# Third-term slices on GpSimd, two more dummy matmuls, folds in sequence and a new order in a two-branch attention kernel

## The chip, the core and the metric

The kernel runs on one core of a Trainium2 chip. The core has five engines with a queue each: TensorE (PE in the profile, its weight loads PEld), VectorE (DVE), ScalarE (ACT), GpSimd (POOL) and SyncE (SP, which here issues nearly all DMAs). They share no order but the semaphores that the program sets. The metric is the device time of one execution in microseconds. Three runs of the kernel before took 785.99, 787.32 and 787.73 us; their median is 787.32.

## What is computed

Two attention layers read the same input x (2048 tokens, 640 features, 32 heads of 20) and are mixed by a gate for each token. Branch A is full softmax attention. In branch B a token sees only the 8 tokens at distances 0, 2, ..., 14 behind it.

```python
g = sigmoid((x * gate_w).sum(-1, keepdims=True))
# A, for each of 32 heads:
p = softmax(q @ k.T * 20**-0.5);  a = (p @ v) joined over the heads @ A_wo
# B, for each head: 8 keys per token, at pos - 0, 2, ..., 14
attn = softmax(q . k[pos - off] * 20**-0.5);  b = (attn . v[pos - off]) joined @ B_wo
out = g * a + (1 - g) * b
```

## The kernel before, in words

**Tiling.** Branch A is cut into 32 groups: 4 chunks of 512 queries (`qc`) by 8 sets of 4 heads (`q`). A group has 16 blocks of 128 keys for each of its 4 heads, so 64 units, each a score block of 128 keys by 512 queries; there are 2048 units in all. `qk` (L1933) lets PE compute the scores of two or three units into PSUM, and `exp` (L1951) lets ScalarE turn these into exponentials in `ebuf` in one instruction; that is a tile, and a step `s` of the main loop. `pv` (L1996) multiplies exponentials by the values (with a column of ones, for the softmax's sum) and accumulates a whole group in the PSUM bank `obank`; four units, one of each head, run side by side in PE.

**Rides: exponentials on VectorE.** Some units do not go to ScalarE. They are taken in quads of up to four (one block of keys, 4 heads). `wanted` decides whether a tile takes such a ride along, or `lone` sends one alone. VectorE then makes a first integer from the score (`clamp`, L1910, result `uD`), whose bits read as bfloat16 are an approximate exponential. To sharpen it, it is summed from K = 4 terms: the term `k` is `uD` plus the constant `SHIFTS[k]` = 0, 32, 64, 96, multiplied by values that are scaled with `WEIGHTS[k]`. The first term is `uD` itself. The other three, k = 1, 2, 3 (second, third and fourth term), are written into slots of `eD`, a ring of `NS` = 3 slots: `gen_d` (L1018, its instruction is L1036) adds the constant on VectorE for all units of a quad at once, one instruction a term. The scaled values `vS` are made on GpSimd (L1082). So a ride costs PE four products in `pv` in place of one. A slot is free again once `pv` has read it.

**Slices on GpSimd.** `piece` (L1050, its instruction is L1065) may take one unit's slice of the second term (k = 1) off VectorE: GpSimd adds the constant as a 32-bit integer addition of `two`, a tile whose one constant, `SHIFTS[1] * 65537`, adds 32 to both 16-bit halves. `pdone` lists which units of a quad are done so, `pshut` remembers that `gen_d` has begun the second term of a quad, so that it is too late for more. `piece` is called by `slot`, after an instruction of VectorE of at least 0.59 us (in the planner's numbers) that reads PSUM or otherwise leaves alone the SBUF port that VectorE shares with GpSimd. If some other work of GpSimd waits for such a slot (`gen_vs`, the norm of a finished group, taps of branch B when `PTAPS` asks for them), that goes first. `last_port` orders the GpSimd instruction behind VectorE's last one that needs the port.

**Side work.** Projections, branch B (`gen_bproj`, `gen_b`), the gate, the norms and the output products are generators. `spend` runs them in the time that PE has left between tiles, through three PSUM banks (`side`), and `filler` (L2017) puts dummy products where PE would be idle. `gen_fold` (L1470) multiplies both branches' results of half a query chunk by the output weights, copies them from PSUM to `outsb` (L1483, L1491) and issues the DMA to the output (L1496). It starts when branch B's half, the output weights and all 8 norms of the chunk are done. There are six; the last chunk goes another way. `close` forces the two folds of the chunk two before to be done.

**What sets the order.** While the program is built, a planner (`_Sched` and the loop at the end of `_build`) keeps an estimated clock for each engine and writes each engine's queue; the waits follow from what is read and written. It decides by 21 settings, which `PLAN` replaces at given steps: slack and tolerances, priorities of the side work, how far VectorE may run ahead, when a ride is taken, and `PTAPS`.

**The head.** `HEAD` is a string that lists the first operations: `t` transposes two blocks of x on PE (L1626), `x` and `y` copy these to SBUF on ScalarE and VectorE (L1636, L1640), `a`, `b`, `k` project the first keys (L1646), and so on up to the first scores. Ahead of it seven dummy matmuls into `obank` (L581) run on zeros.

Of the kernel before, what the change touches and what calls it, by code (L numbers as in the profile page):

```python
# [52 lines left out]
    0: ((0.326, 0.478), 0.16, 1, 1.79, 0.79, -1.26, -0.25, 11.51, 2.0, 9.43, 0.45, 0.67, 3.16, 3.61, -0.03, 0.59, 1, -5.33, 0.3, -1.0, (0, 2)),  # L53
    5: ((0.326, 0.478), 0.16, 1, 1.79, 0.79, -1.26, -0.25, 11.51, 2.0, 9.43, 0.4, 0.67, 3.16, 3.61, -0.03, 0.59, 1, -5.33, 0.3, -1.0, (0, 2)),
    10: ((0.326, 0.478), 0.16, 1, 1.79, 0.79, -1.26, -0.25, 11.51, 3.71, 8.58, 0.4, 0.67, 3.16, 3.61, -0.03, 0.59, 1, -5.33, 0.3, -1.0, (0, 2)),
    15: ((0.381, 0.757), 0.16, 1, 6.06, 0.79, -1.26, -0.25, 11.51, 3.71, 8.58, 0.91, 0.67, 5.31, 4.07, -0.03, 0.59, 2, -5.33, 0.3, -1.0, (0, 2)),
    20: ((0.381, 0.757), 0.16, 2.46, 6.06, 0.79, -1.26, -0.25, 11.51, 3.71, 7.95, 0.91, 0.67, 5.31, 4.07, -0.03, 0.59, 2, -5.33, 0.3, -1.0, (0, 2)),
    25: ((0.381, 0.757), 0.16, 2.46, 6.06, 0.79, -1.26, -0.25, 11.51, 3.71, 6.0, 0.91, 0.67, 5.31, 2.7, -0.03, 0.59, 1, -5.33, 0.3, -1.0, (0, 2)),
    35: ((0.34, 0.55), 0.16, 1.0, 1, 0.69, -1.26, -0.43, 7.8, 4.71, 6.0, 0.91, 0.49, 5.31, 4.29, -0.03, 0.59, 1, -5.33, 0.3, -1.0, (2, 0)),
    40: ((0.34, 0.55), 0.16, 1.0, 1, 0.64, -1.26, -0.43, 7.8, 4.71, 6.0, 0.91, 0.2, 6.33, 4.29, 0.03, 0.59, 1, -5.33, 0.3, -1.0, (2, 2)),  # L60
    45: ((0.34, 0.55), 0.16, 1.0, 1, 0.64, -1.26, -0.13, 7.8, 4.71, 6.0, 0.91, 0.2, 6.33, 4.29, 0.03, 0.59, 1, -5.33, 0.3, -1.0, (2, 2)),
    50: ((0.34, 0.55), 0.16, 1.0, 1, 0.75, -1.26, -0.13, 7.8, 4.71, 6.0, 0.91, 0.2, 6.33, 4.29, 0.03, 0.59, 1, -5.33, 0.3, -1.0, (2, 2)),
    55: ((0.34, 0.55), 0.16, 1.0, 1, 0.75, -1.27, -0.34, 7.8, 4.71, 6.0, 0.91, 0.2, 6.33, 4.29, 0.03, 0.59, 1, -5.33, 0.3, -1.0, (2, 2)),
    60: ((0.421, 0.553), 0.16, 1.0, 1, 0.76, -1.27, -0.34, 7.8, 4.71, 6.0, 0.91, 0.2, 6.33, 4.29, 0.03, 0.59, 1, -5.33, 0.3, -1.0, (2, 2)),
    65: ((0.421, 0.553), 0.16, 1.0, 1, 0.76, -1.27, -0.34, 7.8, 4.71, 6.0, 0.91, 0.2, 6.33, 4.29, 0.1, 0.59, 1, -5.33, 0.3, -1.0, (2, 2)),
    75: ((0.421, 0.553), 0.16, 1.0, 1, 0.76, -1.27, -0.34, 7.8, 1, 6.0, 0.91, 0.2, 6.33, 4.29, 0.1, 0.59, 1, -5.33, 0.3, -1.0, (2, 2)),
    85: ((0.421, 0.553), 0.16, 1.0, 1, 1.14, -1.27, -0.34, 7.8, 7.0, 6.0, 0.91, 0.2, 7.07, 4.29, 0.1, 0.59, 1, -5.33, 0.3, -1.0, (2, 2)),
    95: ((0.421, 0.553), 0.16, 1.0, 1, 1.14, -1.27, -0.34, 7.8, 7.0, 6.0, 0.91, 0.2, 7.07, 4.29, 0.0, 0.59, 1, -5.33, 0.3, -1.0, (2, 2)),
    100: ((0.34, 0.51), 0.39, 1, 1.0, 0.89, -1.26, -0.43, 7.8, 7.0, 9.43, 0.91, 0.32, 5.31, 4.07, 0.08, 0.59, 2, -6, 0.3, -1.0, (2, 2)),
    105: ((0.34, 0.51), 0.25, 1, 1.0, 0.89, -1.26, -0.43, 7.8, 8, 5.03, 0.91, 0.32, 5.31, 3.77, 0.08, 0.59, 2, -6, 0.3, -1.0, (2, 2)),  # L70
    110: ((0.34, 0.51), 0.25, 1, 1.0, 0.89, -1.26, -0.43, 6.8, 8, 5.03, 0.91, 0.32, 5.31, 3.77, 0.08, 0.59, 2, -6, 0.3, -1.0, (2, 2)),
    115: ((0.29, 0.69), 0.25, 1, 1.0, 1.21, -1.26, -0.43, 6.8, 8, 8.57, 0.56, 0.59, 4.37, 3.61, 0.08, 0.73, 2, -3.49, 0.3, -1.0, (2, 2)),
    120: ((0.291, 0.715), 0.39, 1.0, 1.0, 0.94, -1.6, -0.92, 5.92, 2.0, 4.68, 0.64, 0.65, 4.56, 4.29, 0.0, 0.65, 2, -3, 0.3, -1.0, (2, 2)),
    125: ((0.291, 0.715), 0.39, 1.0, 1.0, 0.94, -1.6, -0.92, 5.92, 2.0, 4.68, 0.64, 0.57, 4.56, 4.29, 0.0, 0.65, 2, -3, 0.3, -1.0, (2, 2)),
    130: ((0.291, 0.715), 0.39, 1.0, 1.0, 0.94, -1.6, -0.92, 2, 2.0, 4.68, 0.64, 0.57, 4.56, 4.29, 0.0, 0.65, 2, -3, 0.3, -1.0, (2, 2)),
    140: ((0.291, 0.715), 0.39, 1.0, 1.0, 0.94, -1.6, -0.92, 2, 1, 4.68, 0.53, 0.57, 4.56, 4.29, -0.03, 0.65, 2, -3, 0.3, -1.0, (2, 2)),
    145: ((0.291, 0.715), 0.39, 1.0, 1.0, 1.17, -1.6, -0.92, 2, 1, 4.68, 0.53, 0.57, 4.56, 4.29, -0.03, 0.65, 2, -5.3, 0.3, -1.0, (2, 2)),
    150: ((0.291, 0.715), 0.39, 1.0, 1.0, 1.17, -1.6, -0.92, 2, 1, 4.68, 0.56, 0.57, 4.56, 4.29, -0.03, 0.65, 2, -5.3, 0.3, -1.0, (2, 2)),
# [339 lines left out]
def _build(ctx, nc, A_x, A_wqkv, A_wo, B_wqkv, B_wo, gate_w, out):  # L418
# [66 lines left out]
    kmd4 = small[:, 6:10]  # L485
    KMd = sb([P, CN, 32], BF16, "KMd")
    zero = sb([P, 32], BF16, "zero")
    two = sb([P, 1], I32, "two")
    vw = sb([P, 4], BF16, "vw")
    onesrow = sb([P, 1], FP32, "onesrow")  # L490
    ones2 = sb([P, 2], BF16, "ones2")
# [526 lines left out]
    def gen_d(d):  # L1018
# [6 lines left out]
        for k in range(1, K):  # L1025
# [7 lines left out]
            if k == 1:  # L1033
                pshut[0] = d
# [10 lines left out]
    last_port = lambda: [sch.last_port] if sch.last_port else []  # L1045

    pdone = []
    pshut = [-1]

    def piece(t0):  # L1050

        for d in range(max(0, len(dquads) - 2), len(dquads)):
            if d <= pshut[0] or (closed[d] and not ridden[d]):
                continue
# [1175 lines left out]
```

## Time and profile before

| what | value |
|---|---|
| median of three runs | 787.32 us |
| the profiled execution | 787.67 us |
| its span, first to last instruction | 785.8 us |
| granted clock of PE, mean | 0.999 |
| first exponential starts | 19.74 us |
| tiles (exponential instructions of ScalarE) | 707 |
| rides (clamps of VectorE) | 419 |
| slices of the second term on GpSimd | 182 |

A row of the groups reads: line, engine, operation, what is written from what, shape, number of instructions; after the first bar the busy time in us (overlaps counted once) and the mean duration in ns; after the second the idle time of that engine just before these instructions and what ended it. A row of the timeline reads: start, length in us, then the same. A mean in ns can be longer than an instruction's share of a full engine, since consecutive instructions overlap by about 0.1 us.

### The profile page before, as it was taken

How to read it: one execution, taken by the hardware profiler on the slowest of the kernel's cores; microseconds unless marked ns; L12 is line 12 of the kernel's file. 1: busy time of each engine (PE TensorE's matmuls, PEld its weight loads, DVE VectorE, ACT ScalarE, POOL GpSimd, SP SyncE). 2: the span in 40 equal slices, each digit the busy share in tenths (PEclk: the TensorE clock that was granted, in tenths of full speed). 3: DMA queues.
4: the chain of work that ended last, by engine and by line, in shares of the span. 5: the costliest groups of instructions: out<-in, count | busy, mean ns of one | idle time of the engine just before them, and what ended most of it. 6: DMA issues, size and time to landing. Idle time of an engine off the chain costs nothing.

```text
span 785.8 us, 30107 instructions
## 1 busy us (share of the span) xinstructions
PE 751.9 (96%) x12482; PEld 293.4 (37%) x12483; DVE 699.5 (89%) x1245; ACT 762.3 (97%) x746; POOL 270.4 (34%) x465
## 2 busy tenths in 40 slices
PE   8999999999999999999999999999999999999997
PEld 5432333322233343233334433433343334335333
DVE  5689888999999989997889999999899899996993
ACT  4999999999999999999999999999999999999995
POOL 4124323333543334223334332423234343442220
PEclk9999999999999999999999999999999999999999
DMA  7321221011121142431112401431421241141421
GB/s 228 111 63 39 61 56 37 20 40 28 33 71 35 36 118 54 96 88 29 49 49 66 90 26 54 87 78 33 109 59 28 52 109 43 36 110 41 89 50 35
DMA packets 71454, 49.88 MB, mean 63 GB/s; under 512 B 43096, under 2 KB 64872, under 8 KB 71320
## 3 DMA queue, kind: packets, MB, share of 16 engines
q1 hardware_dynamic: 71032, 47.64, 24.1%
q8 instruction: 99, 1.62, 0.9%
q14 instruction: 35, 0.29, 0.1%
q10 hardware_dynamic: 288, 0.33, 0.1%
HBM read 32.79 MB, written 7.62 MB: 51 GB/s over the span
## 4 chain that ended last, share of the span: by engine, by line
PE 48%; ACT 25%; DVE 14%; issue 12%; DMA 1%; POOL 1%; SPq 0%; DVEq 0%; ACTq 0%; POOLq 0%
ACT ebuf L1951 25%; PE score L1933 14%; PE obank L1996 13%; PE side L685 13%; DVE uD L1910 5%; PE score L685 4%; DVE eD L1036 2%; DVE kvw L1309 1%; DVE qkvB L1138 1%; DMA oTd<-in_A_x_dram 1%; DVE kvw L1200 1%; PE score L1626 1%; PE side L1321 1%; PE score L2017 1%; DVE qkvB L732 0%
## 5 line engine op out<-in xcount | busy, mean ns | idle before, releaser
L1951 ACT ACTIVATE ebuf<-score 128x1024 bf16<-128x1024 f32 (+1 forms) x707 | 749.5, 1207 | 5.2 <-PE score L1933 4.0
L1910 DVE TENSOR_SCALAR uD<-score 128x512 int16<-128x512 f32 x419 | 279.2, 682 | 27.8 <-PE score L1933 26.7
L1933 PE MATMUL score<-qT,kT 32*128 32x512 bf16 x1856 | 257.8, 384 | 17.9 <-ACT ebuf L1951 12.4
L1036 DVE TENSOR_SCALAR eD<-uD 128x2048 int16<-128x2048 int16 (+3 forms) x298 | 185.2, 644 | 4.4 <-PE obank L1996 4.0
L1065 POOL TENSOR_TENSOR eD<-uD,two 128x256 int32<-128x256 int32 x182 | 110.2, 615 | 131.9 <-DVE eD L1036 56.0
L1996 PE MATMUL obank<-ebuf,vA 128*21 128x512 bf16 x1629 | 153.6, 385 | 1.1 <-ACT ebuf L1951 0.7
L1933 PEld LDWEIGHTS score<-qT,kT 32*128 32x128 bf16 x1856 | 63.7, 91 | 210.5 <-ACT ebuf L1951 141.6
L1996 PE MATMUL obank<-eD,vS 128*21 128x512 bf16 x1257 | 109.6, 379 | 0.0
L1082 POOL TENSOR_TENSOR vS<-vA,vw 128x252 bf16<-128x252 bf16 x105 | 65.5, 624 | 124.5 <-DVE eD L1036 54.7
L685 PE MATMUL side<-xT,wBs 128*32 128x256 bf16 x2220 | 89.6, 281 | 1.5 <-DVE rQ L1275 0.7
L685 PEld LDWEIGHTS side<-xT,wBs 128*32 128x32 bf16 x2220 | 63.2, 142 | 28.4 <-issue 15.0
L1008 POOL TENSOR_TENSOR oN<-oTt,oN 128x256 bf16<-128x256 f32 x60 | 44.2, 737 | 74.2 <-DVE eD L1036 49.5
L1996 PEld LDWEIGHTS obank<-ebuf,vA 128*21 128x21 bf16 x1629 | 36.7, 89 | 85.0 <-issue 61.3
L993 POOL TENSOR_TENSOR rcp<-rcp,gA 128x16 f32<-128x16 f32 x30 | 6.7, 223 | 125.7 <-DVE eD L1036 89.6
L1200 DVE TENSOR_TENSOR kvw<-qkvB 128x2048 bf16<-128x2048 bf16 (+2 forms) x40 | 45.2, 1164 | 0.1
L1138 DVE CAST qkvB<-side 128x512 bf16<-128x512 f32 (+1 forms) x67 | 39.1, 593 | 6.3 <-PE side L685 5.9
L1309 DVE TENSOR_TENSOR kvw<-kvw,eB 128x2048 bf16<-128x2048 bf16 (+1 forms) x40 | 44.1, 1118 | 0.6 <-DMA eB<-scr_e 0.6
L1996 PE MATMUL obank<-uD,vA 128*21 128x512 bf16 x419 | 40.8, 379 | 0.0
L1996 PEld LDWEIGHTS obank<-eD,vS 128*21 128x21 bf16 x1257 | 30.8, 91 | 17.6 <-issue 1.6
L685 PE MATMUL side<-xT,WqP 128*32 128x512 bf16 x380 | 29.5, 383 | 0.7 <-DVE xT L1346 0.5
L685 PE MATMUL side<-xT,kvw 128*32 128x512 bf16 (+1 forms) x360 | 29.1, 383 | 0.6 <-DVE oB L732 0.3
L685 PE MATMUL side<-kvw,xT 128*32 128x160 bf16 (+1 forms) x760 | 28.3, 262 | 1.1 <-DVE vA L911 0.4
(207 smaller groups left out, 592.0 us busy)
## 6 DMA issues: line engine op xcount, KB each, us to landing
kvw<-scr_v SPq DMA_DIRECT2D x32, 336.5 KB
oN<-scr_n SPq DMA_DIRECT2D x60, 128.0 KB
scr_v<-qkvB SPq DMA_DIRECT2D x32, 85.0 KB
wBs<-in_B_wqkv_dram SPq DMA_DIRECT2D x5, 480.0 KB
WqP<-in_A_wqkv_dram SPq DMA_DIRECT2D x14, 160.0 KB
oTd<-oN SPq DMA_DIRECT2D x108, 20.0 KB
out_dram<-outsb SPq DMA_DIRECT2D x12, 160.0 KB
qT<-dst SPq DMA_DIRECT2D x93, 20.0 KB
```

The costliest lines, as they stand in the source:

```text
L685: ins = e.matmul(o[j:k, :], l(j) if callable(l) else l[:, j:k], r, start=(first and i == 0), stop=(last and i == n - 1), skip_group_check= ...
L1008: T("pool", 0.73, lambda e, cols=cols: e.tensor_tensor(oN[0][:, cols], oTt[:, cols], rcpR[:, cols], ALU.mult), reads=["oTt", "oN%d" % i], ...
L1036: T("dve", 0.065 + 0.1334 * (n - m), lambda e, k=k, sl=sl, m=m: e.tensor_scalar(eD[:, sl % NS, 512 * m:512 * n].bitcast(I16), uD[d % 2][:, ...
L1065: T("pool", PDUR, lambda e: e.tensor_tensor(eD[:, sl % NS, 512 * i:512 * (i + 1)].bitcast(I32), uD[d % 2][:, 512 * i:512 * (i + 1)].bitcas ...
L1082: T("pool", 0.607, lambda e: e.tensor_tensor(vS[:, d % 2, :, :], _ap(vA, (kb * NQ + q) * 4 * DV, [[0, K - 1], [1, 4 * DV]]), _ap(vw, 0, [[ ...
L1138: t = TB(dvc(n * TOK), lambda e, o=o, i=i: e.tensor_copy(o, i), reads=[("side", b)], writes=[key])
L1200: TB(dvc(n_ * TOK, 2), lambda e: e.tensor_tensor(o, i0, i1, ALU.mult), reads=["qB", "kB"], writes=prods(i, range(n_)) + olds(), port=True)
L1309: TB(dvc(n_ * 2 * TOK, 2), lambda e: e.tensor_tensor(o, i0, i1, ALU.mult), reads=rd, writes=prods(i, range(2 * n_)), port=True)
L1910: t = T("dve", 0.598, lambda e: e.tensor_scalar(uD[d % 2][:, 512 * i:512 * (i + 1)].bitcast(I16), side[x], UOFF, 0.0, op0=ALU.add, op1=ALU ...
L1933: ins = e.matmul(o, kT[32 * j:32 * j + 32, q, kb * P:(kb + 1) * P], qT[qbuf[g]][32 * j:32 * j + 32, :], start=True, stop=True)
L1951: exps[s] = T("act", actc(512 * n), lambda e: e.activation(ebuf[s % NE][:, 0:512 * n], score[s % 2][:, 0:512 * n], ACTF.Exp, scale=LN2 / S ...
L1996: ins = e.matmul(obank[32 * j:32 * j + DV, :], v, src, start=(kb == 0), stop=(last and k >= len(lst) - 4), skip_group_check=True)
```

## The change

`piece` may now take slices of the second and the third term (`KPIECE`), with a list of what is done and a mark that closes it for each term. `two` gets a column for each of the three constants, set by three memsets. Two dummy matmuls (`w`) stand in `HEAD` behind the first transposes. A fold waits until the one before it is done. And all rows of `PLAN` are new, of which two of 126 stand here for all.

```diff
 PLAN = {
-    0: ((0.326, 0.478), 0.16, 1, 1.79, 0.79, -1.26, -0.25, 11.51, 2.0, 9.43, 0.45, 0.67, 3.16, 3.61, -0.03, 0.59, 1, -5.33, 0.3, -1.0, (0, 2)),
+    0: ((0.326, 0.478), 0.0, 1, 1.0, 0.79, -1.09, -0.25, 10.72, 2.0, 9.17, 0.45, 0.36, 3.46, 3.61, 0.0, 0.59, 1, -2.32, 0.3, -1.0, (2, 2)),
...
-    705: ((0.242, 0.809), 0.03, 3.34, 2.69, 1.08, -1.26, -0.43, 13.26, 1.53, 8.57, 0.61, 0.47, 4.5, 4.07, -0.12, 0.71, 2, -7, 0.3, -1.0, (1, 0)),
+    705: ((0.328, 0.562), 0.0, 1.0, 1.0, 1.21, -1.26, -0.43, 7.8, 3.82, 9.37, 0.91, 0.32, 5.3, 4.07, -0.07, 0.59, 1, -2.32, 0.3, -1.0, (0, 2)),
 }
...
-    two = sb([P, 1], I32, "two")
+    two = sb([P, K - 1], I32, "two")
...
-    T("dve", 0.1, lambda e: e.memset(two[:, :], SHIFTS[1] * 65537), writes=["two"])
+    for k_ in range(1, K):
+        T("dve", 0.06, lambda e, k_=k_: e.memset(two[:, k_ - 1:k_], SHIFTS[k_] * 65537), writes=["two"])
...
-            if k > 1 or len(pdone[d]) < n:
-                yield ("dve", DAHEAD, max(sch.free(*[("eD", sl % NS, i) for i in range(n) if k > 1 or i not in pdone[d]]),
+            if len(pdone[d][k]) < n:
+                yield ("dve", DAHEAD, max(sch.free(*[("eD", sl % NS, i) for i in range(n) if i not in pdone[d][k]]),
                                           sch.ready(*[("uD", d % 2, i) for i in range(n)], to="dve")))
-            m = len(pdone[d]) if k == 1 else 0
-            if k == 1:
-                pshut[0] = d
+            m = len(pdone[d][k])
+            pshut.add((d, k))
...
+    KPIECE = (1, 2)
...
-            if d <= pshut[0] or (closed[d] and not ridden[d]):
+            if closed[d] and not ridden[d]:
                 continue
-            sl = sbase[d] if closed[d] else nsl[0]
-            i = len(pdone[d])
...
+            for k in KPIECE:
+                if (d, k) in pshut:
+                    continue
+                sl = (sbase[d] if closed[d] else nsl[0]) + k - 1
+                i = len(pdone[d][k])
+                if npv[0] <= sl - NS or i >= len(ridden[d]) or i >= clamped[d] or ("uD", d % 2, i) not in sch.bufs:
+                    continue
+                if max(sch.avail["pool"], sch.ready(("uD", d % 2, i), to="pool"), sch.free(("eD", sl % NS, i)),
+                       *[x.end + lat(x, "pool") for x in last_port()]) > t0 + PLATE:
+                    continue
+                pdone[d][k].append(i)
+                T("pool", PDUR, lambda e: e.tensor_tensor(
+                    eD[:, sl % NS, 512 * i:512 * (i + 1)].bitcast(I32), uD[d % 2][:, 512 * i:512 * (i + 1)].bitcast(I32),
+                    _ap(two, k - 1, [[0, 256]]), ALU.add), reads=[("uD", d % 2, i)] + ["two"], writes=[("eD", sl % NS, i)],
+                  after=last_port())
+                return
...
     def gen_fold(qc, hu):
+        while qc + hu and not done.get(("fold", *divmod(2 * qc + hu - 1, 2))):
+            yield ("cond",)
...
+              "w": lambda i: T("pe", 0.2, warm_up, reads=[("qabs", 0)], writes=["obank"])}
-    HEAD = ("t0 x0 t1 x1 y0 y1 a0 t2 b0 x2 y2 m0 t3 x3 o0 t4 y3 x4 y4 t5 k1 y5 x5 t6 x6 m1 t7 x7 y6 k2 o1 "
+    HEAD = ("t0 w0 w1 x0 t1 x1 y0 y1 a0 t2 b0 x2 y2 m0 t3 x3 o0 t4 y3 x4 y4 t5 k1 y5 x5 t6 x6 m1 t7 x7 y6 k2 o1 "
             "y7 k3 m2 o2 q0 c0 m3")
```

## The prediction, written before the changed kernel ran

> **What bounds the kernel now.** I read the page's busy shares first, then the groups by line, then busy time by stage.
>
> ```profile
> span 785.8 us, 30107 instructions
> PE 751.9 (96%) x12482; PEld 293.4 (37%) x12483; DVE 699.5 (89%) x1245; ACT 762.3 (97%) x746; POOL 270.4 (34%) x465
> ```
>
> ```profile
> 60.00:760.00 700.00, 675.02 (x11067) 256.35 (x11067) 643.11 (x1106) 695.15 (x678) 252.84 (x431) 1.00 0.24 59
> ```
>
> Columns of the second row: stretch, length, then busy time and instructions of PE, PEld, DVE, ACT and POOL, granted clock, DMA share, GB/s. Between 60 and 760 us ScalarE is idle 4.85 us in 700. Nothing that only fills ScalarE's gaps can matter; the time falls only if ScalarE is given less to do, or if the stretches before its first and after its last exponential shrink. VectorE, at 643.11 of 700 (91.9%), is the other taker of exponential work, and it has 57 us free there. The price list:
>
> ```profile
> L1951 ACT ACTIVATE ebuf<-score 128x1024 bf16<-128x1024 f32 x492 | 474.5, 1079 | 4.3 <-PE score L1933 3.4
> L1951 ACT ACTIVATE ebuf<-score 128x1536 bf16<-128x1536 f32 x215 | 304.3, 1501 | 0.9 <-PE score L1933 0.5
> L1910 DVE TENSOR_SCALAR uD<-score 128x512 int16<-128x512 f32 x419 | 279.2, 682 | 27.8 <-PE score L1933 26.7
> L1036 DVE TENSOR_SCALAR eD<-uD 128x2048 int16<-128x2048 int16 (+3 forms) x298 | 185.2, 644 | 4.4 <-PE obank L1996 4.0
> L1036 DVE TENSOR_SCALAR eD<-uD 128x2048 int16<-128x2048 int16 x237 | 161.3, 696 | 4.2 <-PE obank L1996 4.0
> L1036 DVE TENSOR_SCALAR eD<-uD 128x512 int16<-128x512 int16 x18 | 5.4, 297 | 0.0
> L1065 POOL TENSOR_TENSOR eD<-uD,two 128x256 int32<-128x256 int32 x182 | 110.2, 615 | 131.9 <-DVE eD L1036 56.0 <-PE obank L1996 37.1 <-DVE uD L1910 21.5
> ```
>
> Of 2048 score blocks of 128x512, VectorE takes 419 (the clamps of L1910) and ScalarE 492x2 + 215x3 = 1629. One block costs ScalarE 1501 - 1079 = 0.42 us. A block that VectorE takes, a ride, costs it 279.2/419 + 185.2/419 = 1.11 us: its clamp, and its share of the three further terms that L1036 writes. One slice (one block of one term) costs L1036 (696 - 297)/3 = 0.133 us; GpSimd already takes 182 slices of the second term, 0.615 us each.
>
> **The change, part by part: third-term slices.** Every slice that GpSimd takes gives VectorE 0.133 us. What that is worth: VectorE fills the freed time with rides, each costing 1.11 us and shortening ScalarE's work by 0.42 us. If VectorE keeps its 91.9%, p slices allow x more rides with 0.133 p = x (1.11 + 0.919 x 0.42), so x = 0.089 p, and the time falls by 0.42 x = 0.0375 us for each slice.
>
> How many slices? `piece` runs only beside a VectorE instruction of the clamp's length that leaves the port alone, one GpSimd instruction each. Rows of such instructions, and GpSimd's other uses of such windows:
>
> ```profile
> L1138 DVE CAST qkvB<-side 128x512 bf16<-128x512 f32 x44 | 30.2, 685 | 5.5 <-PE side L685 5.3
> L985 DVE COPY oTt<-obank 128x512 f32<-128x512 f32 x30 | 20.5, 685 | 1.8 <-PE obank L1996 1.0 <-POOL oN L1008 0.6
> L835 DVE TENSOR_SCALAR dst<-side 128x512 bf16<-128x512 f32 x18 | 12.3, 682 | 1.9 <-PE side L685 1.8
> L1082 POOL TENSOR_TENSOR vS<-vA,vw 128x252 bf16<-128x252 bf16 x105 | 65.5, 624 | 124.5 <-DVE eD L1036 54.7 <-DVE kvw L1200 21.1 <-DVE vA L911 18.3
> L1008 POOL TENSOR_TENSOR oN<-oTt,oN 128x256 bf16<-128x256 f32 x60 | 44.2, 737 | 74.2 <-DVE eD L1036 49.5 <-DVE kvw L1200 11.9 <-DMA oN<-scr_n 6.0
> L993 POOL TENSOR_TENSOR rcp<-rcp,gA 128x16 f32<-128x16 f32 x30 | 6.7, 223 | 125.7 <-DVE eD L1036 89.6 <-DVE rcp L989 24.8 <-DVE rQ L1278 6.0
> L1299 POOL TENSOR_TENSOR kvw<-kvw,eB 128x256 bf16<-128x256 bf16 x30 | 19.2, 649 | 11.9 <-DVE kvw L1309 6.3 <-DVE eD L1036 5.0 <-DVE qabs L843 0.6
> L1191 POOL TENSOR_TENSOR kvw<-qkvB 128x256 bf16<-128x256 bf16 x19 | 11.3, 614 | 9.4 <-DVE eD L1036 9.4
> ```
>
> At least 419 + 44 + 30 + 18 = 511 windows, and 182 + 105 + 60 + 30 + 30 + 19 = 426 of them used: 85 free, somewhat more with smaller groups of the same length. Bounds: none (the buffer slot of the third term may still be full: GpSimd already waits 37.1 us for PE's reading of `eD`) and 182, as many as the second term has. I take 100, just above the counted free windows: x = 8.9 rides, -3.75 us; the bounds give 0 and -6.8 us. GpSimd's 61 us more fit into its idle 447 us of the 700.
>
> PE pays for rides: three more products each. Four run abreast:
>
> ```profile
> 400.04 0.40 PE L1996 MATMUL obank<-ebuf,vA 128*21 128x512 bf16 x4
> 400.26 0.39 PE L1996 MATMUL obank<-eD,vS 128*21 128x512 bf16 x4
> L2017 PE MATMUL obank<-xT,zero 128*32 128x512 bf16 x200 | 17.0, 383 | 0.0
> L2017 PE MATMUL score<-xT,ident 128*32 128x512 bf16 x144 | 12.7, 383 | 0.0
> ```
>
> 0.22 us a set, 0.055 each, so 8.9 rides cost PE 1.5 us. The cover is filler: 344 dummy products in these two groups, 86 sets, 19 us that `filler` places only where PE is free. Without that cover the 1.5 us would stand on ScalarE's path.
>
> **Two dummy matmuls after the first transposes.**
>
> ```profile
> 1.22 3.17 PE L581 MATMUL obank<-qabs 128*128 128x512 bf16 x7 [1.22 <-DVE qabs L573]
> 4.18 1.27 PE L1626 MATMUL score<-ident,oTd 128*128 128x128 bf16 x10
> 6.50 1.25 PE L1626 MATMUL score<-ident,oTd 128*128 128x128 bf16 x10 [1.04 <-DMA oTd<-in_A_x_dram]
> 7.54 1.27 PE L1646 MATMUL side<-xT,kvw 128*128 128x256 bf16 x5
> 8.60 1.27 PE L1626 MATMUL score<-ident,oTd 128*128 128x128 bf16 x10
> 9.67 0.75 PE L1646 MATMUL side<-xT,kvw 128*128 128x256 bf16 x5
> 10.26 0.72 PE L1626 MATMUL score<-ident,oTd 128*128 128x128 bf16 x10
> 19.74 14.88 ACT L1951 ACTIVATE ebuf<-score 128x1536 bf16<-128x1536 f32 x14 [0.36 <-PE score L1933]
> ```
>
> The seven of before start (4.18 - 1.22)/7 = 0.42 us apart, so two take 0.85 us, and PE sits idle 1.04 us there, waiting for a DMA. So they are hidden by 0.19 us; were the DMA earlier, they would cost up to 0.85 us. Behind them are queued PE's next transposes, for which ScalarE and VectorE wait. The same ten transposes take 1.27 us until 8.60 and 0.72 from 10.26; the same five products 1.27 and 0.75. PE gets fast about 3.2 us after the idle gap ends, though the page shows the clock as fully granted throughout. If the filled gap makes PE fast at 6.50, the three slow stretches (6.50, 7.54, 8.60) lose 0.53 + 0.52 + 0.55 = 1.6 us, the far bound. Some of it goes to later waits for data before the first exponential at 19.74. I take a third, -0.5 us.
>
> The Trainium skill, "TensorE: Matmul & The Clock Gate", Part 1, says that PE runs at half rate until one free-running window of some 3.4 us has been busy throughout, and falls back after an idle one. The 3.2 us above agree. By it a window reaching over the gap would count as busy once the gap is filled, and the term would be the far bound: the sum below would be 1.1 us lower.
>
> **Two memsets and the folds.** The memset of `two` becomes three of the same kind in the second microsecond, and VectorE's first copy waits there anyway:
>
> ```profile
> 1.56 0.06 DVE L579 MEMSET two<- 128x1 int32 x1
> 5.49 0.56 DVE L1640 COPY xT<-score 128x768 bf16<-128x768 bf16 x1 [2.35 <-PE score L1626]
> 374.32 0.48 DVE L1491 CAST outsb<-score 128x128 bf16<-128x128 f32 x2
> 389.80 0.69 DVE L1483 CAST outsb<-score 128x512 bf16<-128x512 f32 x1 [0.50 <-PE score L685]
> ```
>
> So 0.12 us behind 2.35 us of cover: nothing. The folds are in sequence already in this run: the first's last cast is at 374.32, the second's first at 389.80, and the later folds lie further apart. The rule costs nothing unless the new order brings two together; then a second fold waits some 14 us, still beside other work.
>
> **The new order.** The plan's numbers are replaced at nearly every step, and no row prices that. Averaged over the steps they are of the same kind (from step 200 on, GpSimd's pair of taps of branch B is on in 245 steps, against 270). The bounds come from the stages. Same columns:
>
> ```profile
> 160.00:260.00 100.00, 93.81 (x1342) 31.57 (x1338) 95.77 (x168) 99.80 (x98) 41.39 (x69) 1.00 0.17 41
> 360.00:460.00 100.00, 98.78 (x1703) 39.65 (x1699) 88.47 (x150) 99.46 (x100) 33.73 (x58) 1.00 0.23 56
> ```
>
> If VectorE reached 95.77% in every stage, it would do 700 x 0.9577 - 643.1 = 27 us more; at 0.42/(1.11 + 0.39) = 0.28 us per VectorE us that is -7.6 us. At 88.47% everywhere it is +6.7 us. Between ends so even I take zero.
>
> **The sum.** The profiled execution took 787.67 us: 785.8 of span and 1.87 around it. 787.67 - 3.75 - 0.5 = 783.4 us. That execution was 0.35 us above the median of 787.32, so against medians 783.1 us.
>
> **Rivals.**
> Larger: the new order also brings VectorE nearer to its best stage. Half of the 7.6 us gives 779.3, all of it 775.5. For it: 57 us idle, and slices that lift a constraint on when L1036 runs. Against it: in 360 to 460 PE is at 98.78%, so more rides have little room there.
>
> No change: the third-term slices find their slot of `eD` full or the windows taken. For it: the 37.1 us wait. Against it: the second term found 182. Then only the head is left, 786.8 us.
>
> Slower: the port. GpSimd's piece blocks VectorE's next instruction that needs both of its operand ports. One case:
>
> ```profile
> 413.05 0.73 POOL L1008 TENSOR_TENSOR oN<-oTt,oN 128x256 bf16<-128x256 f32 x1 [1.06 <-DVE eD L1036]
> 413.49 0.44 DVE L843 TENSOR_SCALAR qabs<-dst 128x512 uint16<-128x512 uint16 x1
> L843 DVE TENSOR_SCALAR qabs<-dst 128x512 uint16<-128x512 uint16 x18 | 5.3, 296 | 0.0
> L1036 DVE TENSOR_SCALAR eD<-uD x298: 230/683/1092, 36.7 to 765.6; 128x2048 int16<-128x2048 int16 x118, 128x1024 int16<-128x1024 int16 x12, 128x1536 int16<-128x1536 int16 x12, 128x512 int16<-128x512 int16 x7
> ```
>
> L843 takes 0.44 instead of 0.296 us and ends with the GpSimd instruction: 0.14 us lost, more than the 0.133 that a slice brings. That is the turning point: with 0.14 for each of 100 slices the gain is gone. The longest L1036 took 1092 against a median of 683 ns (the last row: least, median, most), which if it is the port is 0.41 us lost; at the middle, 0.275, VectorE loses 27.5 and gains 13.3 us, and 14.2 x 0.28 = 4 us: about 791 us. At 0.41 for all it is 795. Against it: L1036's four-slice mean of 696 ns is only 13 ns above that median, with 182 such pieces in the run.
>
> The Trainium skill, "SBUF — State Buffer", section on the two separate sides, calls this port pair an exclusive lock held for the whole instruction, with the loser blocked fully. The 0.44 us row agrees.
>
> **How the numbers follow.** Forecast (781 to 785.7) 0.50, larger 0.24, no change 0.09, slower 0.17. A measurement of this kernel tells 0.2%, 1.6 us, from no change. So faster 0.74, same 0.09, slower 0.17. The range runs from within the larger case, 776.5, to the slower one's 791.
>
> **What would show it.** Right: L1065 with some 280 instructions in place of 182, L1910 with 425 to 432, L1951's blocks down by as many, ScalarE still 99% busy in the middle, two more matmuls at about 5.4 us and the next transposes still at 6.5, the ten transposes at 8.60 short. Wrong: L1910 at 419 or fewer, L1036's mean for four slices well above 696 ns, ScalarE idle for PE, or a first exponential later than 19.74 us.

## The result, and the profile after

The changed kernel takes 781.12 us (median of four runs, 780.83 to 781.88) against 787.53 us (four runs) of the kernel before: ratio 0.9924 with a 95% interval of 0.9907 to 0.9941, 6.4 us faster. The prediction said 783.1 us, within 776.5 to 791. One thing is needed to read the size: in the comparisons below the kernel before ran 63 times, and its mean granted clock was 0.999 or more in 37 runs (median 785.95 us) and below it in 26 (median 788.83), while the changed kernel's four runs had 0.999 or more. At equal clock the change is worth 785.95 - 781.12 = 4.8 us; what lies behind the clock's part is in the last section.

The profiled execution took 780.83 us, with a span of 779.0 against 785.8. Its first lines, its groups (same columns as before) and the stretch from 60 to 760 us:

```profile
span 779.0 us, 30108 instructions
PE 747.8 (96%) x12412; PEld 288.3 (37%) x12412; DVE 695.2 (89%) x1245; ACT 758.2 (97%) x749; POOL 333.8 (43%) x570
```

```profile
L1959 ACT ACTIVATE ebuf<-score 128x1024 bf16<-128x1024 f32 x510 | 491.4, 1075 | 2.4 <-PE score L1941 1.4
L1959 ACT ACTIVATE ebuf<-score 128x1536 bf16<-128x1536 f32 x200 | 284.8, 1506 | 0.7 <-PE score L1941 0.6
L1918 DVE TENSOR_SCALAR uD<-score 128x512 int16<-128x512 f32 x428 | 287.2, 681 | 34.5 <-PE score L1941 32.1
L1037 DVE TENSOR_SCALAR eD<-uD 128x2048 int16<-128x2048 int16 (+3 forms) x287 | 171.7, 620 | 5.7 <-PE obank L2004 5.0
L1037 DVE TENSOR_SCALAR eD<-uD 128x2048 int16<-128x2048 int16 x203 | 137.1, 692 | 5.5 <-PE obank L2004 5.0
L1068 POOL TENSOR_TENSOR eD<-uD,two 128x256 int32<-128x256 int32 x288 | 173.6, 617 | 116.8 <-DVE eD L1037 53.7 <-DVE kvw L1314 18.3 <-DVE uD L1918 16.7
```

```profile
60.00:760.00 700.00, 676.90 (x11166) 255.84 (x11162) 642.77 (x1105) 696.82 (x683) 309.18 (x525) 1.00 0.24 59
```

The lines have moved by a few: `exp` is L1959 now, `clamp` L1918, `qk` L1941, `pv` L2004, `gen_d` L1037, `piece` L1068. GpSimd takes 288 slices instead of 182 (92 of the third term, as the experiments show, and 14 more of the second), VectorE 428 rides instead of 419, ScalarE 510x2 + 200x3 = 1620 blocks instead of 1629. VectorE is as busy as before (642.77 of 700 us against 643.11): it spends the freed time on rides, and its four-slice instruction takes 692 ns against 696, with 1.6 times as many slices on GpSimd.

The head, on PE (the first five rows) and on ScalarE:

```profile
4.18 0.86 PE L1633 MATMUL score<-ident,oTd 128*128 128x128 bf16 x10
4.88 0.59 PE L583 MATMUL obank<-qabs 128*128 128x512 bf16 x2
6.81 0.73 PE L1633 MATMUL score<-ident,oTd 128*128 128x128 bf16 x10 [1.33 <-DMA oTd<-in_A_x_dram]
7.38 0.71 PE L1653 MATMUL side<-xT,kvw 128*128 128x256 bf16 x5
7.93 0.72 PE L1633 MATMUL score<-ident,oTd 128*128 128x128 bf16 x10
```

```profile
18.52 3.31 ACT L1959 ACTIVATE ebuf<-score 128x1536 bf16<-128x1536 f32 x3 [0.37 <-PE score L1941]
...
759.63 10.14 ACT L1959 ACTIVATE ebuf<-score 128x1024 bf16<-128x1024 f32 x9
```

The first exponential starts at 18.52 us instead of 19.74, the last ends at 759.63 + 10.14 = 769.77. The first ten transposes already take 0.86 us here, where they took 1.27 before: PE became fast in the middle of them, ahead of the first dummy at 4.88.

**A ledger for ScalarE.** The mean duration of an exponential isn't its price when ScalarE works without a break. Two pairs of rows of the kernel before, each pair with the same start, show the distance between ends:

```profile
388.82 2.41 ACT L1951 ACTIVATE ebuf<-score 128x1536 bf16<-128x1536 f32 x2
...
388.82 10.66 ACT L1951 ACTIVATE ebuf<-score 128x1536 bf16<-128x1536 f32 x11
...
756.28 3.09 ACT L1951 ACTIVATE ebuf<-score 128x1536 bf16<-128x1536 f32 x2
...
756.28 20.55 ACT L1951 ACTIVATE ebuf<-score 128x1536 bf16<-128x1536 f32 x15
```

Between the second and the eleventh end lie nine two-block tiles: (10.66 - 2.41)/9 = 0.917 us each, where the mean duration is 1.079. Between the second and the fifteenth lie thirteen three-block tiles: (20.55 - 3.09)/13 = 1.343 us, mean duration 1.501. (A merged row prints only the shape of its first instruction.) Over the whole trace the medians of these distances are the same, 0.917 and 1.343. The difference of 0.426 us is the price of a block, as the prediction had it; the rest of a duration, 0.16 us (more than the 0.1 us given with the profile before), lies under the instruction before. The Trainium skill, "Perfetto Trace Analysis", section "Optimizing Scalar/DVE Operations", says that the fixed access cost of an instruction shows about doubled in a profiled latency, and that the write-acknowledgement half of it overlaps with the next instruction; this trace agrees that there is such an overlap, though its 0.16 us is above the page's figures for ScalarE, 51 ns on PSUM and 93 ns on SBUF.

So the pure work is 492 x 0.917 + 215 x 1.343 = 739.9 us before and 510 x 0.917 + 200 x 1.343 = 736.3 after. The exponentials reach from 19.74 to 756.28 + 20.55 = 776.83 before (757.1 us) and from 18.52 to 769.77 after (751.3 us). What is not work on exponentials, the rest, is 17.2 and 15.0 us. ScalarE's 21 other instructions in that stretch are 6.0 and 6.4 us of it, from end to end; the other 11 and 9 us are lateness. The 6.8 us of span are then 3.6 of less work, 2.2 of less rest, 1.2 of an earlier start, and 0.2 lost in the tail (785.8 - 776.83 = 9.0 against 9.2).

### The profile page after: what moved, and what is told of

The parts are those of the page before. It is cut to its first block, busy times and chain, and to the rows that moved or that the text cites. A ratio compares the mean times of both kernels' runs of the same rounds, so it can differ in the third digit from the quotient of the medians.

```text
span 779.0 us, 30108 instructions
## 1 busy us (share of the span) xinstructions
PE 747.8 (96%) x12412; PEld 288.3 (37%) x12412; DVE 695.2 (89%) x1245; ACT 758.2 (97%) x749; POOL 333.8 (43%) x570
## 4 chain that ended last, share of the span: by engine, by line
PE 49%; ACT 27%; issue 11%; DVE 11%; DMA 2%; SPq 0%; POOL 0%; DVEq 0%; ACTq 0%
ACT ebuf L1959 27%; PE score L1941 15%; PE obank L2004 14%; PE side L687 12%; PE score L687 4%; DVE uD L1918 3%; DVE eD L1037 2%; DVE kvw L1314 1%; DVE qkvB L1143 1%; DVE kvw L1205 1%; DMA woBp<-in_B_wo_dram 1%; PE side L1218 1%; DMA oTd<-in_A_x_dram 1%; PE side L1326 1%; DMA scr_q<-qbnd 0%
## 5 line engine op out<-in xcount | busy, mean ns | idle before, releaser
L1959 ACT ACTIVATE ebuf<-score 128x1024 bf16<-128x1024 f32 (+1 forms) x710 | 745.2, 1197 | 3.1 <-PE score L1941 2.0
L1918 DVE TENSOR_SCALAR uD<-score 128x512 int16<-128x512 f32 x428 | 287.2, 681 | 34.5 <-PE score L1941 32.1
L1941 PE MATMUL score<-qT,kT 32*128 32x512 bf16 x1856 | 259.0, 384 | 12.7 <-ACT ebuf L1959 9.2
L1068 POOL TENSOR_TENSOR eD<-uD,two 128x256 int32<-128x256 int32 x288 | 173.6, 617 | 116.8 <-DVE eD L1037 53.7
L1037 DVE TENSOR_SCALAR eD<-uD 128x2048 int16<-128x2048 int16 (+3 forms) x287 | 171.7, 620 | 5.7 <-PE obank L2004 5.0
L2004 PE MATMUL obank<-ebuf,vA 128*21 128x512 bf16 x1620 | 153.3, 385 | 0.3
L1941 PEld LDWEIGHTS score<-qT,kT 32*128 32x128 bf16 x1856 | 64.0, 91 | 210.4 <-ACT ebuf L1959 149.8
L2004 PE MATMUL obank<-eD,vS 128*21 128x512 bf16 x1284 | 110.8, 380 | 0.4 <-POOL eD L1068 0.3
L687 PE MATMUL side<-xT,wBs 128*32 128x256 bf16 x2400 | 97.4, 281 | 2.9 <-DVE qkvB L1143 1.4
L687 PEld LDWEIGHTS side<-xT,wBs 128*32 128x32 bf16 x2400 | 68.4, 141 | 33.9 <-issue 15.4
L2004 PEld LDWEIGHTS obank<-ebuf,vA 128*21 128x21 bf16 x1620 | 36.8, 89 | 83.6 <-issue 62.4
L1143 DVE CAST qkvB<-side 128x512 bf16<-128x512 f32 (+1 forms) x72 | 42.1, 594 | 4.5 <-PE side L687 4.2
L2004 PE MATMUL obank<-uD,vA 128*21 128x512 bf16 x428 | 41.5, 379 | 0.0
L2004 PEld LDWEIGHTS obank<-eD,vS 128*21 128x21 bf16 x1284 | 30.8, 91 | 20.2 <-DVE eD L1037 2.3
L1941 PE MATMUL score<-woBp,kT 32*128 32x512 bf16 x192 | 30.0, 384 | 0.5
```

Source lines behind the costliest of these rows:

```text
L687: ins = e.matmul(o[j:k, :], l(j) if callable(l) else l[:, j:k], r, start=(first and i == 0), stop=(last and i == n - 1), skip_group_check= ...
L1037: T("dve", 0.065 + 0.1334 * (n - m), lambda e, k=k, sl=sl, m=m: e.tensor_scalar(eD[:, sl % NS, 512 * m:512 * n].bitcast(I16), uD[d % 2][:, ...
L1068: T("pool", PDUR, lambda e: e.tensor_tensor(eD[:, sl % NS, 512 * i:512 * (i + 1)].bitcast(I32), uD[d % 2][:, 512 * i:512 * (i + 1)].bitcas ...
L1143: t = TB(dvc(n * TOK), lambda e, o=o, i=i: e.tensor_copy(o, i), reads=[("side", b)], writes=[key])
L1918: t = T("dve", 0.598, lambda e: e.tensor_scalar(uD[d % 2][:, 512 * i:512 * (i + 1)].bitcast(I16), side[x], UOFF, 0.0, op0=ALU.add, op1=ALU ...
L1941: ins = e.matmul(o, kT[32 * j:32 * j + 32, q, kb * P:(kb + 1) * P], qT[qbuf[g]][32 * j:32 * j + 32, :], start=True, stop=True)
```

## The experiments

In nearly all of them the operations that the planner issued (engine, function, reads, writes) were recorded, edited, and issued again in the same order, with the waits worked out anew. So an edit acts alone, without the planner answering to it.

| kernel | median us (runs) | ratio to before, 95% |
|---|---|---|
| before_w | 786.27 (12) | 0.9974 to 1.0009 |
| after_no_w | 782.05 (6) | 0.9907 to 0.9956 |
| after_third_back | 786.04 (12) | 0.9968 to 0.9999 |
| after_both_back | 802.28 (4) | 1.0163 to 1.0221 |
| before_36_less | 785.69 (10) | 0.9962 to 0.9997 |
| before_slices_out | 786.10 (10) | 0.9974 to 1.0006 |
| before_slices_and_36 | 783.26 (10) | 0.9938 to 0.9970 |
| before_36_less_no_fill | 781.61 (4) | 0.9892 to 0.9950 |
| before_all_three | 782.25 (5) | 0.9925 to 0.9961 |
| after_no_fill | 781.28 (4) | 0.9883 to 0.9942 |
| after_no_fold_rule | 804.40 (1) | |
| after_old_settings | 856.66 (1) | |

### The two dummies, alone and undone

Into the kernel before, behind its first transposes:

```diff
+            if e[1] == ("t", 0):
+                for i in range(2):
+                    out.append([-2, None, ("pe", 0.2, warm_up), dict(reads=[("qabs", 0)], writes=["obank"], after=[])])
```

> The kernel before, every queue in its own order, with the two dummy matmuls put behind the first transposes and nothing else changed. Theory (the filled gap makes PE fast by about 6.8 us instead of 9.7): first exponential 1.2 us earlier, at 18.5, and about 786.2 us. Rival (PE gets fast at a moment that has nothing to do with the dummies, and differs from execution to execution): first exponential as often near 19.7 as near 18.5, and the median within 0.5 us of before.

Out of the changed one:

```diff
+        return [e for e in log if e[1] != ("w",)]
```

> The changed kernel without the two dummy matmuls, every queue otherwise in the changed kernel's order. Theory: PE slow until about 9.7 us, first exponential at 19.7, about 782.3 us against 781.1. Rival (PE gets fast without them as well): 781.1 us, first exponential at 18.5.

PE at the start of the kernel before with dummies, its first exponential, and one later stretch (columns as in the prediction's stretches):

```profile
4.18 1.27 PE L1652 MATMUL score<-ident,oTd 128*128 128x128 bf16 x10
5.25 0.75 PE L607 MATMUL obank<-qabs 128*128 128x512 bf16 x2
6.04 0.73 PE L1652 MATMUL score<-ident,oTd 128*128 128x128 bf16 x10
```

```profile
17.97 4.67 ACT L1978 ACTIVATE ebuf<-score 128x1536 bf16<-128x1536 f32 x4 [0.36 <-PE score L1960]
```

```profile
700.00:720.00 20.00, 19.38 (x289) 7.71 (x282) 10.97 (x18) 17.69 (x20) 5.46 (x11) 0.83 0.22 56
```

And the changed kernel without them:

```profile
6.54 1.25 PE L1664 MATMUL score<-ident,oTd 128*128 128x128 bf16 x10 [1.09 <-DMA oTd<-in_A_x_dram]
7.58 1.27 PE L1684 MATMUL side<-xT,kvw 128*128 128x256 bf16 x5
8.65 1.27 PE L1664 MATMUL score<-ident,oTd 128*128 128x128 bf16 x10
```

```profile
20.17 2.36 ACT L1994 ACTIVATE ebuf<-score 128x1536 bf16<-128x1536 f32 x2 [0.36 <-PE score L1976]
```

These two executions say what the theory said: with dummies PE is fast at 6.04 us, without them still slow at 8.65. But two executions don't make a rule. The first exponential in all fourteen profiled executions, with how long the second set of ten transposes took:

| with the two dummies | start us | transposes us | without | start us | transposes us |
|---|---|---|---|---|---|
| after | 18.52 | 0.73 | before | 19.74 | 1.25 |
| before_w | 17.97 | 0.73 | after_no_w | 20.17 | 1.25 |
| after_third_back | 17.99 | 0.73 | before_36_less | 17.79 | 0.73 |
| after_both_back | 18.20 | 0.73 | before_slices_out | 18.14 | 0.73 |
| after_no_fill | 18.71 | 0.73 | before_slices_and_36 | 19.01 | 0.73 |
| after_no_fold_rule | 17.93 | 0.73 | before_36_less_no_fill | 17.54 | 0.73 |
| after_old_settings | 17.92 | 0.73 | before_all_three | 18.32 | 0.73 |

With dummies seven of seven were fast, without them five of seven. The means are 18.18 and 18.67 us, 0.5 apart. A slow head costs about 1.8 us (the two slow ones average 19.96, the other five without dummies 18.16), and what else moves the start is when the DMA brings the second piece of x: the second transposes start between 5.83 and 7.30 us. In four executions with dummies (after, after_both_back, after_no_fill, after_old_settings) PE was fast before the first dummy began, so these say nothing about them; in four of those without, too, it was fast before the first ten transposes were over. Of the six that were left, all three with dummies were fast at the second transposes, and one of three without. In the times nothing certain is left: before_w is level with before, after_no_w 0.9 us above the changed kernel. So it isn't settled whether the dummies do anything; no cost of them shows.

### The slices put back on VectorE

```diff
+    BACK = (2,)       # after_both_back: (1, 2)
+            if tag and tag[0] == "piece" and tag[2] in BACK:
+                continue
+            if tag and tag[0] == "d" and tag[2] in BACK:
+                _, d, k, sl, n = tag
...
+                e = [idx, None, ("dve", 0.065 + 0.1334 * n, fn), kw]
```

`fn` is `gen_d`'s instruction for all `n` units of the quad.

> The changed kernel in its own order with its 428 rides, but the 92 third-term slices are back in VectorE's instructions. VectorE gets 92 x 0.133 = 12 us more to do. If VectorE's idle time takes this up (it has 50 us idle between 60 and 753 us), the time stays within 2 us of 781.1. If, in a fixed order, VectorE paces the kernel as much as ScalarE does, the time rises by most of the 12 us, to 788 to 793 us. A gain of the slices that had nothing to do with VectorE would leave 781.1.

> As the run before, with the 196 second-term slices back on VectorE too, so that GpSimd takes none: VectorE gets 288 x 0.133 = 38 us more. Taken up by idle time: at most 50 us are there, so 785 or less. VectorE paces: 810 to 819 us. If the price of one slice is the same over the whole range, three times the rise of the run before.

Busy times and GpSimd's remaining slices with the third term back, and busy times with both back:

```profile
PE 749.0 (96%) x12411; PEld 288.7 (37%) x12412; DVE 706.0 (90%) x1256; ACT 760.1 (97%) x749; POOL 281.2 (36%) x478
```

```profile
L1099 POOL TENSOR_TENSOR eD<-uD,two 128x256 int32<-128x256 int32 x196 | 119.6, 619 | 108.3 <-DVE eD L1067 33.5 <-DVE uD L1949 19.1 <-DVE kvw L1345 14.0
```

```profile
PE 753.2 (94%) x12411; PEld 288.5 (36%) x12412; DVE 730.4 (91%) x1279; ACT 765.4 (96%) x749; POOL 160.9 (20%) x282
```

So 288 - 196 = 92 of the slices are of the third term. They give VectorE 706.0 - 695.2 = 10.8 us of work back, and the time rises by 4.9 us, to that of the kernel before (786.04 us, all runs at a clock of 0.999 or more, against 785.85 for such runs of the kernel before beside them). All 288 give it 35.2 us, and the time rises by 21.2. That is 0.45 and 0.60 us for each us of VectorE, or 0.053 us for a slice of the third term. Both times lie between the two theories: VectorE's idle time takes up a part of the burden. Nor is the price the same over the whole range, since 21.2 us is more than three times 4.9. In this order, then, the rides bring their gain only with the slices on GpSimd. Whether a newly planned order without third-term slices could have brought it too was not run.

### Relief in the order of before

The prediction's argument was that ScalarE sets the pace. Then taking work off ScalarE, with every queue's order kept, must show in full. Three reliefs, alone and together: 36 three-block exponentials write only two blocks; 92 third-term instructions of `gen_d` leave out their last unit; all 106 sets of `filler` are left out (the prediction's two groups held 86 of them).

```diff
+        three = [e for e in log if e[1] and e[1][0] == "exp" and e[1][2] == 3 and e[1][1] >= 60][::5][:36]
+        for e in three:
+            s = e[1][1]
+            e[2] = ("act", actc(1024), lambda e_, s=s: e_.activation(
+                ebuf[s % NE][:, 0:1024], score[s % 2][:, 0:1024], ACTF.Exp, scale=LN2 / STEP))
```

> The kernel before in its own order; in 36 three-block tiles ScalarE computes two blocks only, so 36 of its 1629 exponentials are left out (the products read what the buffer held). VectorE, GpSimd and PE have the same work. Theory (ScalarE's work paces the kernel, 0.42 us a block): 36 x 0.42 = 15 us less, about 772 us. Rival (in a given order PE's and VectorE's queues are as tight as ScalarE's, so that a block less for ScalarE alone is mostly waited away): 784 to 786 us, with ScalarE idle by some 13 us more.

```diff
+            if e[1] and e[1][0] == "d" and e[1][2] == 2 and e[1][1] >= 4 and n2 < 92:
...
+                e[2] = ("dve", 0.065 + 0.1334 * (n - 1), lambda e_, k=k, sl=sl, d=d, n=n: e_.tensor_scalar(
+                    eD[:, sl % NS, 0:512 * (n - 1)].bitcast(I16), uD[d % 2][:, 0:512 * (n - 1)].bitcast(I16), SHIFTS[k], None, op0=ALU.add))
```

> The kernel before in its own order; in 92 of VectorE's third-term instructions one slice is left out (the products read what the slot held), 92 x 0.133 = 12 us less for VectorE, all else the same. Theory (ScalarE paces; VectorE's time is worth something only when rides take its place): 786 to 787 us, no change. Rival (VectorE's queue paces in a fixed order, as it did when the changed kernel got 92 slices back): 782 to 783 us.

> Both of the two runs before: 36 exponentials fewer on ScalarE and 92 slices fewer on VectorE. If the two engines pace the kernel together, more than the sum of the two gains, and up to 12 us in all: 775 to 779 us. If ScalarE alone paces: 772, as with the exponentials alone. If PE's queue paces: 785 or more.

```diff
+        return [e for e in log if e[1] != ("fill",)]
```

> The kernel before with 36 of ScalarE's exponentials left out, and with PE's 106 filler sets (23 us) left out too. With the exponentials alone left out the time fell by 1 us in place of 15. If the fillers in PE's queue held it back, 772 to 778 us. If it is the order of the real work of PE and VectorE, 784 to 786 us, as with the fillers.

> The kernel before in its own order with all three engines relieved: 36 of ScalarE's exponentials left out (15 us), one slice left out of 92 of VectorE's third-term instructions (12 us), PE's 106 filler sets left out (23 us). If the three queues pace together and nothing else, about the 12 to 15 us that the least relieved of them gives: 772 to 775 us. If the gains only add up (6 with exponentials and fillers, 2.4 more for the slices beside the exponentials): 779 us. If the order itself (which product stands before which in PE's queue) holds, no less than 781.

The busy times of before_36_less, its groups of ScalarE (L1978 the untouched exponentials, L2233 the 36), and the first and last of them:

```profile
PE 750.1 (96%) x12483; PEld 292.1 (37%) x12483; DVE 698.7 (89%) x1245; ACT 753.9 (96%) x746; POOL 270.1 (35%) x465
```

```profile
L1978 ACT ACTIVATE ebuf<-score 128x1024 bf16<-128x1024 f32 x492 | 473.8, 1055 | 8.0 <-PE score L1959 5.4
L1978 ACT ACTIVATE ebuf<-score 128x1536 bf16<-128x1536 f32 x179 | 255.1, 1481 | 2.5 <-PE score L1959 1.6
L2233 ACT ACTIVATE ebuf<-score 128x1024 bf16<-128x1024 f32 x36 | 38.2, 1061 | 0.1
```

```profile
17.79 2.37 ACT L1978 ACTIVATE ebuf<-score 128x1536 bf16<-128x1536 f32 x2 [0.37 <-PE score L1959]
...
768.11 4.22 ACT L1978 ACTIVATE ebuf<-score 128x1536 bf16<-128x1536 f32 x3
```

ScalarE lost 36 x 0.426 = 15.3 us of work, and the median fell by 1.0 us (by 2.2, from 786.16 to 783.99, between runs at a clock of 0.999 or more). By the ledger: 528 x 0.917 + 179 x 1.343 = 724.6 us of work between 17.79 and 772.33, so 29.9 us of rest where there were 17.2 (its other instructions are 6.6 us of it). Yet the idle time that the rows show has only gone from 5.2 to 10.6 us, and ScalarE still shows as 96% busy. The other half of the waiting is in the durations: where ScalarE waits for PE, the overlap with the instruction before is lost, the means fall (1079 to 1055 and 1501 to 1481 ns), and of the 15.3 us of work taken away the busy time shows only 762.3 - 753.9 = 8.4. The chains of waits, before first, say the same:

```profile
PE 48%; ACT 25%; DVE 14%; issue 12%; DMA 1%; POOL 1%; SPq 0%; DVEq 0%; ACTq 0%; POOLq 0%
```

```profile
PE 55%; ACT 17%; DVE 16%; issue 8%; DMA 2%; SPq 1%; POOL 0%; DVEq 0%; ACTq 0%
```

PE held half of the chain from the start, and takes over what ScalarE gives up. The ledgers of the others, worked out in the same way from the start of the first and the end of the last exponential:

| kernel | first to last us | work us | rest us |
|---|---|---|---|
| before | 757.1 | 739.9 | 17.2 |
| after | 751.3 | 736.3 | 15.0 |
| after_third_back | 756.1 | 736.3 | 19.8 |
| after_both_back | 772.9 | 736.3 | 36.6 |
| before_slices_out | 757.2 | 739.9 | 17.3 |
| before_36_less | 754.5 | 724.6 | 29.9 |
| before_slices_and_36 | 754.6 | 724.6 | 30.0 |
| before_36_less_no_fill | 752.7 | 724.6 | 28.1 |
| before_all_three | 751.6 | 724.6 | 27.0 |

The busy times of before_slices_out:

```profile
PE 750.4 (96%) x12483; PEld 292.1 (37%) x12483; DVE 689.7 (88%) x1245; ACT 762.2 (97%) x746; POOL 269.1 (34%) x465
```

VectorE has 9.8 us less to do than in before (699.5), and nothing moved: 17.3 us of rest for 17.2, and a median 0.6 us lower, inside its interval. ScalarE and VectorE together gave 3.4 us; ScalarE with the fillers out 6.0 and all three 4.9, which four and five runs don't tell apart. That fits PE standing behind ScalarE, as the chain has it, but doesn't show it: the fillers alone were not taken out of the kernel before, so how much of the 6.0 us is theirs is open. With work off all three engines 27 us of rest remain. PE's products for the scores, in before and in before_all_three, show one side of it:

```profile
L1933 PE MATMUL score<-qT,kT 32*128 32x512 bf16 x1856 | 257.8, 384 | 17.9 <-ACT ebuf L1951 12.4 <-DVE uD L1910 2.8 <-DVE qT L1732 0.2
L1960 PE MATMUL score<-qT,kT 32*128 32x512 bf16 x1856 | 258.4, 385 | 22.3 <-ACT ebuf L1979 14.7 <-DVE uD L1937 3.4 <-DVE qkvB L1165 0.8
```

PE waits for ScalarE's exponentials (12.4 and 14.7 us) while ScalarE waits for PE's scores: the two take turns. That the order in which the queues are served holds the rest of the 27 us is likely; which waits end last there was not followed.

### Cover and settings

The same edit, all sets of `filler` left out, on the changed kernel:

> The changed kernel in its own order without any of the 81 sets of filler products, 0.22 us each, 18 us of PE's time. If fillers are only slack (placed where PE is free), the time stays at 781.1 within 0.5 us. If PE's queue paces in a fixed order and fillers stand in it, some us less, 775 to 780. If PE's speed depends on them, slower: some 1.7 us for each window of 3.4 us at half speed.

The first lines of its page:

```profile
span 779.0 us, 29473 instructions
...
PE 734.5 (94%) x12088; PEld 282.2 (36%) x12088; DVE 694.6 (89%) x1245; ACT 757.4 (97%) x749; POOL 331.4 (43%) x570
```

Without its (12412 - 12088)/4 = 81 sets of filler PE is 13.3 us less busy, and the time is the same, 781.28 us: the filler of the new order is slack for the time, as the prediction used it.

The last two let the planner decide again: without the fold rule (the diff), and with the rule but with all rows of `PLAN` as before:

```diff
-        while qc + hu and not done.get(("fold", *divmod(2 * qc + hu - 1, 2))):
-            yield ("cond",)
```

> The changed kernel planned without the rule that a fold waits for the one before it, all settings the same. If the rule never decides anything, the queues come out the same and so does the time, 781. If the plan's course depends on it (the settings were made for the course with the rule), the queues differ, fewer rides are taken, and it is slower than 781 by 0.42 us for each ride missing and more where work is left to the end: 785 to 800 us.

> The changed kernel (third-term slices allowed, dummies, fold rule) planned with the settings of the kernel before. If the slices alone bring the gain, 782 to 785 us. If settings and rules only fit together (the run without the fold rule lost 23 us), far slower than before: fewer rides than 419 and 800 us or more.

The span and the groups of rides and slices of after_no_fold_rule, then of after_old_settings:

```profile
span 802.6 us, 30214 instructions
```

```profile
L1916 DVE TENSOR_SCALAR uD<-score 128x512 int16<-128x512 f32 x411 | 276.1, 684 | 50.1 <-PE score L1939 48.5
L1068 POOL TENSOR_TENSOR eD<-uD,two 128x256 int32<-128x256 int32 x250 | 151.2, 618 | 131.6 <-DVE eD L1037 62.1 <-PE obank L2002 24.1 <-DVE uD L1916 17.2
```

```profile
span 854.9 us, 30143 instructions
```

```profile
L1917 DVE TENSOR_SCALAR uD<-score 128x512 int16<-128x512 f32 x382 | 257.0, 685 | 65.4 <-PE score L1940 63.5
L1067 POOL TENSOR_TENSOR eD<-uD,two 128x256 int32<-128x256 int32 x223 | 135.9, 622 | 102.3 <-DVE eD L1036 41.7 <-DVE uD L1917 24.2 <-PE obank L2003 15.2
```

Both are single runs. The settings act at given steps. Whatever changes what has been issued by a step makes the later settings act on a state that they weren't found for: fewer rides, fewer slices, and clamps that wait longer for PE's scores (50.1 and 65.4 us, against 34.5). So "the slices alone" can't be had by giving the changed code its old settings, and what the new settings add by themselves wasn't separated.

## Why the prediction was right, point by point

**Slices, rides and their price: right.** 106 more slices were foreseen as 100 (all of the third term; 92 are), 9 more rides as 8.9, 3.6 us of ScalarE's work as 3.75. VectorE's busy share stayed as assumed. That the slices pay for the rides in this order is shown by after_third_back: same rides, slices back, and the gain is gone.

**"The time falls only if ScalarE is given less to do": this step failed**, though the sum built on it came out. It was read from 4.85 us of idle time in 700. That number is too small: before_36_less hides over half of its added waiting in durations, and the ledger finds 11 us of lateness in before. Nor does the time follow ScalarE's work: a relief of 15.3 us was worth 1.0 to 2.2, and after_third_back and after_both_back, with ScalarE's work unchanged at 736.3 us, were 4.9 and 21.2 us slower. ScalarE and PE wait for each other, and VectorE's load counts too. That the 0.426 us a block were earned in the new order, where the planner placed the 9 rides and PE's products together, fits the times; no run shows it by itself. The chain's 48% for PE stood on the page and was not read.

**The new order at zero: too small by 2.2 us** in the profiled pair, the fall of the rest from 17.2 to 15.0, well inside the bounds of -7.6 and +6.7; no run separates it from the other parts. Part of that is the pair and not the change: the profiled execution of before, 787.67 us, lay 1.7 above the median of its runs at full clock. At equal clock the change brought 4.8 us, against the sum's 3.75 + 0.5 = 4.25.

**The dummies at -0.5 us: right in size, not in the picture.** They were hidden as worked out, and the clock's gain was taken as a third of 1.6 us because later waits would eat the rest. The runs give another reason for about the same number: a slow head does cost some 1.8 us, but without dummies it came in two of seven executions only, and in the changed kernel's profiled execution PE was fast before the dummies ran. So the 1.2 us by which its first exponential is earlier are not shown to be theirs, and that half a microsecond came out is luck. The rule of the Trainium skill ("TensorE: Matmul & The Clock Gate", Part 1), by which the far bound would hold, is right for the execution that was looked at; the same section says that the window runs freely, so that the moment varies from run to run. These heads agree in that, but not in the size: it gives 500 ns either way for unbroken work, while here, from the same seven matmuls at 1.22 us and with waits for a DMA between, PE became fast between 4.0 and 10.7 us. One profile of before couldn't show that.

**Slower by the port: refuted.** The four-slice instruction takes 692 ns with 288 slices against 696 with 182; the prediction's rival needed at least 140 ns lost for each of 100 slices, which over the 203 four-slice instructions would be some 70 ns more each. The one case it read is off in a detail: GpSimd's instruction ends at 413.05 + 0.73 = 413.78 us, VectorE's at 413.49 + 0.44 = 413.93, so they don't end together.

**The fold rule at nothing: right for the engines, wrong for the plan.** In the changed kernel the folds lie in sequence at no visible cost; but with the rule taken out, the planner goes another way and ends 23 us later (one run).

**The larger and the no-change rivals** were 779.3 us or less and 786.8; 781.12 lies at the lower edge of the forecast's own range, 781 to 785.7.

## What to carry to other kernels

An engine that shows as 99% busy isn't thereby the one that sets the pace. Work out its pure work from the distance between ends where it runs without a break, and read the chain of waits beside the busy shares: what lies between that work, with the engine's other instructions, and the elapsed time is waiting, however little idle time is shown. In a program whose queues are ordered beforehand, a freed microsecond can be worth little until the order is made anew for it, and a burdened one can cost at once (9.8 us taken off VectorE in the kernel before brought 0.6, within the noise, while each us put on it in the changed one cost 0.45 to 0.60); so judge such a change with its order, and an experiment on one part with the order held.

## What the runs showed of the hardware

**A dip of the granted clock within some executions.** In the profile of before_w the mean clock is 0.83 between 700 and 720 us (row above) and 1.00 in the stretches beside it; ScalarE did 17.69 us of work in these 20, and the span is 786.8 us. In finer stretches (columns as before) it is half the clock for 6.8 us:

```profile
698.50:701.90 3.40, 2.11 (x28) 0.62 (x29) 3.40 (x6) 3.40 (x5) 1.83 (x4) 1.00 0.22 70
701.90:705.30 3.40, 3.40 (x34) 0.77 (x30) 1.98 (x3) 2.49 (x3) 1.43 (x3) 0.50 0.41 107
705.30:708.70 3.40, 3.40 (x44) 1.03 (x44) 1.29 (x4) 2.46 (x3) 0.00 (x0) 0.50 0.08 18
```

In the 3.4 us before the dip PE was busy for 2.11 us only. The same stands before the dips of before_slices_out (2.11 of 3.4 us, dip at 700.4), before_slices_and_36 (2.11, at 698.7), after_both_back (1.97, at 434.2), before_all_three (2.37 and 2.07, at 318.7 and 752.2) and after_no_fill (1.99 and 1.97, at 748.5 and 755.3), which last 3.4 us each. So a lull of PE goes ahead of the dip; in before's own profile PE was busy for 2.73 us in that stretch, and the clock stayed full. Not every lull brings a dip: in before_36_less_no_fill PE was busy for some 2.2 us of the 3.4 from 737.7 on, and none followed. The 63 runs of before have medians 2.9 us apart on the two sides of a mean clock of 0.999 (784.98 to 788.31 us, and 786.99 to 791.10). The 22 runs of the changed kernel, after_no_w and after_third_back all had 0.999 or more, so the dips that the new order didn't have may be part of its gain: 1.6 of the 6.4 us. Two of the four runs of after_both_back had 0.997; the four of after_no_fill had 0.991 to 0.998 and lost nothing by it. Why the lull comes in some executions only is open.

**Occupancy and waiting.** The Trainium skill, "Perfetto Trace Analysis", section "Identifying the Most-Contended Engine", takes the occupancy of ScalarE as a fair measure of how near it is to its limit. Here it reads 97% before and 96% in before_36_less, while the work fell by 15.3 us and the rest rose by 12.7: the measurement decides against it where instructions overlap.

**GpSimd beside VectorE.** 288 integer additions of 128x256, 617 ns each, stood beside VectorE instructions without lengthening its instruction for the slices (692 ns for four slices, 696 before).
